# Sketched attention and a mixture of attention experts on one core: sketch matrices decoded ahead of the block transposes, products formed bank by bank, and ten extra matmuls at the start

## The chip, the cores and the metric

One core of one Trainium2 chip runs the kernel. The metric is the time of one execution on the device, in microseconds (us), as the median of several runs. A profile is a trace of one execution. The engines are TensorE (PE; PEld is its weight load), VectorE (DVE), ScalarE (ACT), GpSimd (POOL) and SyncE (SP), which only issues transfers (DMAs); ACT and POOL issue some too. Each engine takes its instructions strictly in the order in which they stand in its own queue.

## The reference

Batch is 4, there are 4 heads, 1088 tokens, head width 32. `S1` and `S2` are two 8 x 32 sketch matrices in double precision; everything else is float32.

```python
def phi(x):                                   # x: one head, S1 and S2 project 32 -> 8
    a = np.einsum('rd,bhsd->bhsr', S1, x)
    b = np.einsum('rd,bhsd->bhsr', S2, x)
    return np.einsum('bhsi,bhsj->bhsij', a, b).reshape(*x.shape[:-1], 64)
q_p, k_p = phi(q), phi(k)
kv = einsum('bhsf,bhsd->bhfd', k_p, v);  z = k_p.sum(axis=2)
x  = (q_p @ kv) / (q_p @ z + 1e-6)            # heads side by side: (B, 1088, 128)
# four experts on x, top 2 of 4 by the logits x @ w_gate, softmax weights w:
for e in range(4):
    a  = softmax(causal(scale * (x @ wq[e]) @ (x @ wk[e]).T))
    out += gate(w, e) * (a @ (x @ wv[e]) @ wo[e])
```

## The kernel before, in words

**Tiling.** A batch is 1088 tokens in NJ = 9 blocks of 128 (the last has 64). Its inputs are `kin`, `qin`, `vin` and `vtl`. VectorE turns `kin` and `qin` in 32 x 32 squares into `kT` and `qT` (L220 to L223: 1024 columns of k, the last 64 columns of k, all of q). `SKW` is the sketch matrix that both are multiplied with: a 128-row block-diagonal matrix, one 32-row block for each head, in two float32 parts (NS = 2), a high and a low one.

**Sketch.** `sketch` (L228) takes four blocks to one PSUM bank, so k and q have three banks each (4, 4 and 1 blocks): matmuls into `kps` or `qps` (L235), a copy by ScalarE of the high part into `kab` or `qab` (L239), and VectorE's addition of the low part (L241). One float32 matmul is two passes in the trace.

**Products.** After all three banks, `products` (L243) forms the 64 features of each token and head: one instruction per head of 128 x 576 elements into `kp` or `qp` (L248). In batch 0 VectorE has three of the four of k and two of q, GpSimd the others; in batches 1 to 3 GpSimd has all.

**Rest of the preparation.** `kvs` (L265) multiplies `kp` with v (copied to `vp` by GpSimd, L217) to `kv`; `turn_features` (L278) transposes `qp` on TensorE into `tq`, evacuated to `qpT`; `numer` (L287) multiplies `qpT` with `kvz` to `num`; VectorE divides (L292 to L294) to `xs`; `turn_x` (L302) transposes to `tx`, evacuated to `xT`. `project` (L312) then makes the experts' `qk` out of `xT`.

**Attention.** For each batch, units of scores, softmax, transposes, values and output follow (`units`). `gates` (L461) has GpSimd make `rb`, which TensorE transposes as `rt` (L468) before values can be scaled. TensorE's order is written out by hand (`manual_schedule`): the pieces of the next batch's preparation are strewn between the units by costs that add up. The other engines' order is set by the tile scheduler, which places each instruction by its own estimate of when it can run. `prepare(0)` runs with nothing to overlap it.

**Start.** The sketch matrices arrive as 64-bit numbers in `S_raw`, 16 rows for each of four heads, in eight small transfers (L116, four from ACT's queue and four from POOL's). VectorE decodes each double into two floats in 19 short integer and float operations (L130 to L151), turns the result to `ST` (L160) and multiplies by a block mask `blk` to `SKW` (L162).

Of the kernel before, what the change touches and what calls it, by code (L numbers as in the profile page):

```python
# [3 lines left out]

# [15 lines left out]
def kernel(  # L20
# [38 lines left out]
    def const(name, shape, dt=F32):  # L59
        return cp.tile(shape, dt, name=name, tag=name)  # L60
# [35 lines left out]


    NS = 1 if S1.dtype == F32 else 2
    S_sum = const("S_sum", [128, NS, 32])
    blk = const("blk", [128, H])  # L100
    nc.gpsimd.memset(blk, 0.0)
    for h in range(H):
        nc.gpsimd.memset(blk[32 * h : 32 * h + 32, h : h + 1], 1.0)
    if NS == 1:
        nc.vector.memset(S_sum, 0.0)
        for x, s in enumerate((S1, S2)):
            for h in range(H):
                nc.scalar.dma_start(out=S_sum[32 * h + R * x : 32 * h + R * x + R, 0, :], in_=s)
        load(0)
    else:  # L110
        raw = const("S_raw", [128, 32, 2], I32)
        nc.vector.memset(raw, 0)
        for x, s in enumerate((S1, S2)):
            for h in range(H):
                eng = (nc.scalar, nc.gpsimd)[h % 2]
                eng.dma_start(out=raw[32 * h + R * x : 32 * h + R * x + R].rearrange("p d w -> p (d w)"),  # L116
                              in_=s.bitcast(I32))
        load(0)

# [38 lines left out]
    ST = const("ST", [128, NS, 32])  # L158
    SKW = const("SKW", [128, NS, 2, H, R])
    nc.vector.transpose(ST.rearrange("p n d -> p (n d)"), S_sum.rearrange("p n d -> p (n d)"))  # L160
    for n in range(NS):
        nc.vector.tensor_tensor(  # L162
            out=SKW[:, n], in0=ST[:, n, 0 : 2 * R].rearrange("p (x r) -> p x r", x=2)[:, :, None, :].to_broadcast([128, 2, H, R]),
            in1=blk[:, None, :, None].to_broadcast([128, 2, H, R]), op=ALU.mult)
    NB = 8 // NS

    nc.gpsimd.memset(kT[:, S:], 0.0)
# [33 lines left out]
    def prepare(b):  # L201
# [14 lines left out]
        def begin():  # L216
            nc.gpsimd.tensor_copy(vp[:, 0:n, :, 0:D].rearrange("p j h d -> p h j d"), vin)  # L217
            nc.gpsimd.tensor_copy(vp[0:64, n, :, 0:D], vtl)

            nc.vector.transpose(kT[:, 0 : 128 * n].rearrange("p (j g t) -> p j g t", j=n, g=4),  # L220
                                kin[:, 0 : 128 * n].rearrange("p (g j d) -> p j g d", g=4, j=n))
            nc.vector.transpose(kT[:, 128 * n : S], kin[:, 128 * n : S])
            nc.vector.transpose(qT[:, 0:S], qin)  # L223
            if b + 1 < B:
                load(b + 1)

        def sketch(nm, xT_, j0):

            if nm not in abS:
                abS[nm] = p2.tile([128, NJ, 64], F32, tag="ab", name=f"{nm}ab{b}")  # L230
            j1 = min(j0 + NB, NJ)
            w = 64 * NS
            t = bank(f"{nm}ps{b}_{j0}")
            for j in range(j0, j1):
                nc.tensor.matmul(t[:, w * (j - j0) : w * (j - j0) + w], xT_[:, 128 * j : 128 * j + 128],  # L235
                                 SKW.rearrange("p s x h r -> p (s x h r)"), start=True, stop=True)
            t = t[:, 0 : w * (j1 - j0)].rearrange("p (j s m) -> p j s m", s=NS, m=64)
            ab = abS[nm][:, j0:j1]
            nc.scalar.copy(ab, t[:, :, 0])  # L239
            if NS == 2:  # L240
                nc.vector.tensor_tensor(out=ab, in0=ab, in1=t[:, :, 1], op=ALU.add)  # L241

        def products(nm, engines):  # L243

            fp = p2.tile([128, NJ, H, R * R], F32, tag="fp", name=f"{nm}p{b}")
            f4 = abS[nm].rearrange("p j (x h r) -> p j x h r", x=2, r=R)
            for h in range(H):
                engines[h].tensor_tensor(  # L248
                    out=fp[:, :, h].rearrange("p j (x y) -> p j x y", y=R),
                    in0=f4[:, :, 1, h, None, :].to_broadcast([128, NJ, R, R]),  # L250
                    in1=f4[:, :, 0, h, :, None].to_broadcast([128, NJ, R, R]),
                    op=ALU.mult)
            fps[nm] = fp
# [30 lines left out]
        def numer(g):  # L284
            num = bank(f"num{b}_{g}")
            for y in range(6):
                nc.tensor.matmul(num[:, 66 * y : 66 * y + 66], qpT[:, 6 * g + y],  # L287
                                 kvz[:, y % 2].rearrange("p h d -> p (h d)"), start=True, stop=True)
            nu = num[:, 0 : 12 * (D + 1)].rearrange("p (m d) -> p m d", d=D + 1)
            den = p2.tile([128, 12], F32, tag="den", name=f"den{b}_{g}")  # L290
            xs = p2.tile([128, 3, 128], F32, tag="xs", name=f"xs{b}_{g}", bufs=3)
            nc.vector.tensor_scalar_add(den, nu[:, :, D], 1e-6)  # L292
            nc.vector.reciprocal(den, den)
            nc.vector.tensor_tensor(  # L294
                out=xs.rearrange("p x (h d) -> p (x h) d", d=D), in0=nu[:, :, 0:D],
                in1=den[:, :, None].to_broadcast([128, 12, D]), op=ALU.mult)
# [55 lines left out]
        V, G = nc.vector, nc.gpsimd  # L352
        kq, qq = ([V, V, V, G], [V, G, V, G]) if first else ([G] * H, [G] * H)
        wait = (0.9, None)
        sk = {nm: [(0.9, lambda j=j, nm=nm, t=t: sketch(nm, t, j)) for j in range(0, NJ, NB)]
              for nm, t in (("k", kT), ("q", qT))}
# [5 lines left out]
        pieces = [(0.0, begin)] + sk["k"] + [(0.0, lambda: products("k", kq))]  # L362
        pieces += sk["q"] + [(0.0, lambda: products("q", qq)), wait, (2.0, lambda: (kvs(0), kvs(1))), wait, wait]
        pieces += tq[0:3] + nu[0:1] + tq[3:4] + nu[1:2] + tq[4:5] + tx[0:1] + nu[2:3] + tx[1:2] + [wait] + tx[2:3]
        rest = pr[1] + [(0.5, project_tails)]
        if first:
# [292 lines left out]
```

## Time and profile before

| what | us |
|---|---|
| median of 3 runs | 433.3 (432.59 to 437.13) |
| the profiled execution, its own time | 433.48 |
| span of that execution, first to last instruction | 430.9 |
| TensorE busy | 394.8 (92% of the span) |
| VectorE, ScalarE, GpSimd busy | 234.2, 225.3, 63.4 |

The time of an execution is the span and 2.6 us around it. The page gives the span in 40 slices; in the first slice TensorE is idle, and its granted clock, `PEclk`, reads below 10 tenths in the third and fourth slice. A row of the chain of waits has a start, a duration and a name: it is followed back from the last instruction, at each step to what released it. A matmul's own duration includes its way through the array; matmuls in a row overlap, so what one costs is the duration of a row divided by its count.

### The profile page before, as it was taken

Reading aid. Unit: us, or ns where it says so; the run is one execution under the profiler, and the core shown is the slowest. Engines: PE = TensorE matmul, PEld = TensorE weight load, DVE = VectorE, ACT = ScalarE, POOL = GpSimd, SP = SyncE. Lnnn points to the kernel's source line nnn. Section 1 sums busy time; section 2 is a strip of 40 time slices with the busy share of each in tenths; the row PEclk is TensorE's granted clock in tenths of the full one; section 3 lists DMA queues with packets and bytes.
Section 4 is the critical chain, followed back from the end, with each engine's and each line's share of the span. In section 5 each row is a group of like instructions: output and inputs, shape, how many; then the busy total and the mean of one; then the engine's idle time right before and its main releaser. Section 6 shows DMA issues by size and latency. Waiting matters only on the chain.

```text
span 430.9 us, 8172 instructions
## 1 busy us (share of the span) xinstructions
PE 394.8 (92%) x3264; PEld 272.0 (63%) x3264; DVE 234.2 (54%) x495; ACT 225.3 (52%) x564; POOL 63.4 (15%) x99
## 2 busy tenths in 40 slices
PE   0678999999999998999999999999999998999995
PEld 0674676775665765686566576777666575666663
DVE  3673665663675454556355545555566355544552
ACT  1122655556655544565564535656664564566662
POOL 4240036000000046000000018000000000000110
PEclk9988999999999999999999999999999999999999
DMA  7532012100000000000000000000000000000000
GB/s 209 152 116 41 2 52 86 33 14 0 2 13 2 14 5 14 0 14 2 1 14 1 9 9 2 14 0 14 0 14 2 0 14 5 0 14 5 2 12 26
DMA packets 11510, 9.98 MB, mean 23 GB/s; under 512 B 3792, under 2 KB 10448, under 8 KB 11472
## 3 DMA queue, kind: packets, MB, share of 16 engines
q1 hardware_dynamic: 9280, 8.92, 7.4%
q10 hardware_dynamic: 2064, 0.53, 0.6%
q8 instruction: 25, 0.41, 0.4%
q14 instruction: 13, 0.11, 0.1%
q0 software_dynamic: 128, 0.01, 0.0%
HBM read 7.23 MB, written 2.23 MB: 22 GB/s over the span
## 4 chain that ended last, share of the span: by engine, by line
PE 74%; ACT 9%; DVE 8%; issue 3%; POOL 3%; DMA 2%; ACTq 0%; POOLq 0%; DVEq 0%
PE sc L390 17%; PE tp L445 14%; PE av L508 13%; PE qk L312 7%; ACT a L376 7%; PE num L287 3%; PE sc L393 3%; PE po L551 3%; PE kps L235 2%; PE vg L324 2%; PE tq L278 2%; PE av L537 2%; PE sc L413 2%; DVE mx L400 2%; PE rt L468 1%
## 5 line engine op out<-in xcount | busy, mean ns | idle before, releaser
L376 ACT ACTIVATE a<-sc,mx 128x1024 f32<-128x1024 f32 (+7 forms) x136 | 103.1, 763 | 87.3 <-DVE mx L400 47.9
L445 PE MATMUL tp<-ident,a 128*128 128x128 f32 (+1 forms) x648 | 95.1, 277 | 6.3 <-ACT a L376 4.8
L400 DVE TENSOR_REDUCE mx<-sc 128x1 f32<-128x640 f32 (+3 forms) x64 | 62.6, 1019 | 49.0 <-PE sc L393 49.0
L72 ACT COPY aT<-tp 128x512 f32<-128x512 f32 (+1 forms) x122 | 63.2, 540 | 45.6 <-PE tp L445 45.2
L445 PEld LDWEIGHTS tp<-ident,a 128*128 128x128 f32 (+1 forms) x648 | 71.4, 141 | 22.2 <-ACT a L376 9.4
L390 PE MATMUL sc<-qkT 64*128 64x512 f32 (+3 forms) x384 | 80.9, 518 | 0.8 <-ACT a L376 0.8
L508 PE MATMUL av<-aT,vt 128*64 128x256 f32 (+1 forms) x640 | 69.2, 363 | 0.0
L461 POOL TENSOR_TENSOR rb<-gw,r 128x256 f32<-128x256 f32 (+1 forms) x36 | 21.2, 590 | 322.4 <-DVE r L458 253.7
L508 PEld LDWEIGHTS av<-aT,vt 128*64 128x64 f32 x640 | 42.9, 137 | 21.7 <-issue 0.2
L390 PEld LDWEIGHTS sc<-qkT 64*128 64x128 f32 x384 | 32.2, 185 | 31.3 <-issue 26.2
L70 DVE COPY aT<-tp 128x512 f32<-128x512 f32 (+2 forms) x58 | 37.8, 652 | 16.5 <-PE tp L445 15.9
L397 DVE TENSOR_REDUCE mx<-sc 128x2 f32<-128x256 f32 (+3 forms) x32 | 26.2, 820 | 21.8 <-PE sc L393 21.8
L312 PE MATMUL qk<-xT,wqk 128*128 128x512 f32 x64 | 33.0, 632 | 0.9 <-ACT xT L72 0.8
L376 ACT ACTIVATION_READ_ACCUMULATOR a<-sc,mx 128x1 f32 x136 | 27.1, 199 | 0.0
L393 PEld LDWEIGHTS <-identb 128*128 128x128 bf16 x128 | 7.3, 97 | 28.1 <-issue 26.2
L235 PE MATMUL kps<-SKW,kT 128*128 128x128 f32 x72 | 11.7, 317 | 14.2 <-DVE SKW L162 14.2
L324 PE MATMUL vg<-wvg,xT 128*128 128x260 f32 (+1 forms) x72 | 21.4, 396 | 1.1 <-DVE vt L70 0.5
L551 PE MATMUL po<-wo,yT 128*128 128x128 f32 (+1 forms) x144 | 20.5, 282 | 1.3 <-ACT aT L72 0.8
L510 DVE TENSOR_TENSOR yT<-av,rs 128x256 f32<-128x256 f32 x32 | 13.5, 422 | 13.5 <-PE av L508 13.4
L235 PEld LDWEIGHTS kps<-SKW,kT 128*128 128x128 f32 x72 | 10.6, 226 | 14.5 <-DVE SKW L162 14.2
L551 PEld LDWEIGHTS po<-wo,yT 128*128 128x128 f32 (+1 forms) x144 | 17.5, 185 | 3.2 <-ACT aT L72 1.1
L248 POOL TENSOR_TENSOR kp<-kab 128x576 f32<-128x576 f32 x13 | 15.5, 1221 | 24.9 <-DVE kab L241 21.6
(117 smaller groups left out, 415.9 us busy)
## 6 DMA issues: line engine op xcount, KB each, us to landing
kin<-in_k_dram SPq DMA_DIRECT2D x4, 544.0 KB, 3.6
qin<-in_q_dram SPq DMA_DIRECT2D x4, 544.0 KB, 6.0
vin<-in_v_dram SPq DMA_DIRECT2D x16, 128.0 KB, 3.1
out_dram<-ob SPq DMA_DIRECT2D x16, 128.0 KB, 1.8
wqk<-in_moe_wq_dram ACTq DMA_DIRECT2D x1, 128.0 KB, 4.9
wqk<-in_moe_wk_dram ACTq DMA_DIRECT2D x1, 128.0 KB, 5.0
wvg<-in_moe_wv_dram ACTq DMA_DIRECT2D x1, 128.0 KB, 3.1
wo<-in_moe_wo_dram ACTq DMA_DIRECT2D x1, 128.0 KB
```

Of the source, the lines that this page charges most:

```text
L70: nc.vector.tensor_copy(out_, in_)
L72: nc.scalar.copy(out_, in_)
L235: nc.tensor.matmul(t[:, w * (j - j0) : w * (j - j0) + w], xT_[:, 128 * j : 128 * j + 128], SKW.rearrange("p s x h r -> p (s x h r)"), star ...
L312: nc.tensor.matmul(t, wt(a), xT[:, 512 * c : 512 * c + 512], start=True, stop=True)
L324: nc.tensor.matmul(t[0:m, 0 : E * HD + E], xT[:, 128 * j : 128 * j + m], wvg, start=True, stop=True)
L376: nc.scalar.activation(out=dst, in_=src, func=ACTF.Exp, bias=mx, accum_out=z)
L390: nc.tensor.matmul(sc[e][:, c0:c1], qk[rows, g, 128 * i : 128 * i + 128], qk[rows, NG + g, c0:c1], start=True, stop=(c1 < n))
L397: nc.vector.tensor_reduce(mx, t[:, :, 0:n], axis=AX.X, op=ALU.max, negate=True)
L400: nc.vector.tensor_reduce(mx[:, e : e + 1], sc[e][:, 0:n], axis=AX.X, op=ALU.max, negate=True)
L445: nc.tensor.transpose(tp[0:nk, k - k0, :], ats[e][:, 128 * j : 128 * j + nk], ident)
L508: nc.tensor.matmul(av[HD * e : HD * e + HD, lo:256], vt[:, j, c : c + HD], aT[:, 2 * j + e, lo:256], start=(j == 0), stop=(j == 2 * p + 1))
L551: nc.tensor.matmul(po[0:nq, DM * x : DM * x + DM], yT[:, g, 128 * x : 128 * x + nq], wo_sb[:, g], start=(g == 0), stop=(g == NG - 1))
```

## The change

The sketch matrices come in two transfers, not eight, one from SP's queue and one from ACT's, into 32 rows, and the decode works on 32 partitions where it worked on 128. `SKW` is set to zero by GpSimd and its four diagonal blocks are copied out of `ST`, two by VectorE and two by GpSimd; `blk` is gone. A scheduling bound, `issue_after(mark[0])`, holds the block transposes of batch 0 behind the turn to `ST`, and those of batch 1 behind the last division `xs` of batch 0. The products are made in `sketch`, at the end of each bank and for all heads at once (128 x 1024 elements for a bank of four blocks, 128 x 256 for the last): by VectorE alone in batch 0, by GpSimd alone after it. `kab` and `qab` have their two halves apart (`[128, 2, NJ, 32]`). Ten matmuls of `ident` with itself, which nothing reads, stand at the head of TensorE's order.

```diff
-    S_sum = const("S_sum", [128, NS, 32])
-    blk = const("blk", [128, H])
-    nc.gpsimd.memset(blk, 0.0)
-    for h in range(H):
-        nc.gpsimd.memset(blk[32 * h : 32 * h + 32, h : h + 1], 1.0)
...
-        raw = const("S_raw", [128, 32, 2], I32)
-        nc.vector.memset(raw, 0)
-        for x, s in enumerate((S1, S2)):
-            for h in range(H):
-                eng = (nc.scalar, nc.gpsimd)[h % 2]
-                eng.dma_start(out=raw[32 * h + R * x : 32 * h + R * x + R].rearrange("p d w -> p (d w)"),
-                              in_=s.bitcast(I32))
-        load(0)
+    S_sum = const("S_sum", [32, NS, 32])
+    raw = S_sum.rearrange("p n d -> p (n d)") if NS == 1 else const("S_raw", [32, 32, 2], I32)
+    nc.vector.memset(raw, 0.0 if NS == 1 else 0)
+    for x, s in enumerate((S1, S2)):
+        eng = (nc.sync, nc.scalar)[x]
...
+            eng.dma_start(out=raw[R * x : R * x + R].rearrange("p d w -> p (d w)"), in_=s.bitcast(I32))
+    load(0)
...
-    nc.vector.transpose(ST.rearrange("p n d -> p (n d)"), S_sum.rearrange("p n d -> p (n d)"))
-    for n in range(NS):
-        nc.vector.tensor_tensor(
-            out=SKW[:, n], in0=ST[:, n, 0 : 2 * R].rearrange("p (x r) -> p x r", x=2)[:, :, None, :].to_broadcast([128, 2, H, R]),
-            in1=blk[:, None, :, None].to_broadcast([128, 2, H, R]), op=ALU.mult)
+    nc.gpsimd.memset(SKW, 0.0)
+
+    mark = [nc.vector.transpose(ST.rearrange("p n d -> p (n d)"), S_sum.rearrange("p n d -> p (n d)")).ins]
+    for h in range(H):
+        (nc.vector, nc.gpsimd)[h % 2].tensor_copy(
+            SKW[32 * h : 32 * h + 32, :, :, h, :], ST[:, :, 0 : 2 * R].rearrange("d n (x r) -> d n x r", x=2))
...
-            nc.vector.transpose(kT[:, 0 : 128 * n].rearrange("p (j g t) -> p j g t", j=n, g=4),
+            with tc.issue_after(mark[0]) if b < 2 else nullcontext():
+                nc.vector.transpose(kT[:, 0 : 128 * n].rearrange("p (j g t) -> p j g t", j=n, g=4),
...
-                abS[nm] = p2.tile([128, NJ, 64], F32, tag="ab", name=f"{nm}ab{b}")
+                abS[nm] = p2.tile([128, 2, NJ, H * R], F32, tag="ab", name=f"{nm}ab{b}")
+                fps[nm] = p2.tile([128, NJ, H, R * R], F32, tag="fp", name=f"{nm}p{b}")
...
-        def products(nm, engines):
...
-            for h in range(H):
-                engines[h].tensor_tensor(
-                    out=fp[:, :, h].rearrange("p j (x y) -> p j x y", y=R),
...
+            ab = ab.rearrange("p x j (h r) -> p x (j h) r", r=R)
+            n = H * (j1 - j0)
+            (nc.vector if first else nc.gpsimd).tensor_tensor(
+                out=fps[nm][:, j0:j1].rearrange("p j h (x y) -> p (j h) x y", y=R),
+                in0=ab[:, 1, :, None, :].to_broadcast([128, n, R, R]),
+                in1=ab[:, 0, :, :, None].to_broadcast([128, n, R, R]),
+                op=ALU.mult)
...
-            nc.vector.tensor_tensor(
+            last = nc.vector.tensor_tensor(
                 out=xs.rearrange("p x (h d) -> p (x h) d", d=D), in0=nu[:, :, 0:D],
                 in1=den[:, :, None].to_broadcast([128, 12, D]), op=ALU.mult)
+            if first:
+                mark[:] = [last.ins]
...
-        kq, qq = ([V, V, V, G], [V, G, V, G]) if first else ([G] * H, [G] * H)
...
     with tc.manual_schedule(engines={mybir.EngineType.PE}):
+
+        warm = ps_tp.tile([128, 512], F32, tag="tp", name="warm")
+        for _ in range(10):
+            nc.tensor.matmul(warm[:, 0:128], ident, ident, start=True, stop=True)
```

VectorE's queue at the start, before: the decode (`S_` names) stands between the transposes of k and q (five of its 19 operations are shown).

```order
L198 TENSOR_SCALAR wqk<-wqk 128x256
L220 STREAM_TRANSPOSE kT<-kin 128x1024
L132 TENSOR_SCALAR S_ex<-S_raw 128x32
...
L222 STREAM_TRANSPOSE kT<-kin 128x64
L132 TENSOR_SCALAR S_ex<-S_ex 128x32
L135 TENSOR_TENSOR S_ma<-S_ma,S_lw 128x32
L223 STREAM_TRANSPOSE qT<-qin 128x1088
L130 TENSOR_SCALAR S_ex<-S_ex 128x32
...
L135 TENSOR_TENSOR S_sum<-S_lead,S_last 128x32
L160 STREAM_TRANSPOSE ST<-S_sum 128x64
L162 TENSOR_TENSOR SKW<-ST,blk 128x64 x2
```

The same place now, where the whole decode and `ST` come first:

```order
L190 TENSOR_SCALAR wqk<-wqk 128x256
L123 TENSOR_SCALAR S_ex<-S_raw 32x32
...
L126 TENSOR_TENSOR S_sum<-S_lead,S_last 32x32
L153 STREAM_TRANSPOSE ST<-S_sum 32x64
L213 STREAM_TRANSPOSE kT<-kin 128x1024
L155 COPY SKW<-ST 32x4x8 x2
L215 STREAM_TRANSPOSE kT<-kin 128x64
L216 STREAM_TRANSPOSE qT<-qin 128x1088
```

The long transpose of k moved behind the decode, ahead of the two copies into `SKW`; the transpose of q moved behind everything that the first sketch matmul needs.

VectorE's queue at batch 0's products, before; the transposes in it belong to batch 1.

```order
L241 TENSOR_TENSOR kab_189<-kab_189,kps_8_204 128x64
L248 TENSOR_TENSOR kp_208<-kab_189 128x9x64 x3
L241 TENSOR_TENSOR qab_213<-qab_213,qps_0_214 128x256
L241 TENSOR_TENSOR qab_213<-qab_213,qps_4_221 128x256
L241 TENSOR_TENSOR qab_213<-qab_213,qps_8_228 128x64
L220 STREAM_TRANSPOSE kT<-kin 128x1024
L248 TENSOR_TENSOR qp_232<-qab_213 128x9x64 x2
L222 STREAM_TRANSPOSE kT<-kin 128x64
L223 STREAM_TRANSPOSE qT<-qin 128x1088
L70 COPY qpT_175<-tq_8_288 128x512
```

The same place now:

```order
L235 TENSOR_TENSOR kab_191<-kab_191,kps_0_193 128x2x128
L235 TENSOR_TENSOR kab_191<-kab_191,kps_4_201 128x2x128
L239 TENSOR_TENSOR kp_192<-kab_191 128x1024 x2
L235 TENSOR_TENSOR kab_191<-kab_191,kps_8_209 128x2x32
L235 TENSOR_TENSOR qab_214<-qab_214,qps_0_216 128x2x128
L239 TENSOR_TENSOR kp_192<-kab_191 128x256
L239 TENSOR_TENSOR qp_215<-qab_214 128x1024
L235 TENSOR_TENSOR qab_214<-qab_214,qps_4_224 128x2x128
L235 TENSOR_TENSOR qab_214<-qab_214,qps_8_232 128x2x32
L239 TENSOR_TENSOR qp_215<-qab_214 128x1024
L239 TENSOR_TENSOR qp_215<-qab_214 128x256
L70 COPY qpT_177<-tq_8_288 128x512
```

Batch 1's transposes left this place for one behind the last `xs` of batch 0, just ahead of the copy of the first `qk` bank. The first product of k stands behind the sums of two banks, not of one.

GpSimd's queue in batch 1, before:

```order
L461 TENSOR_TENSOR rb_0_1_546<-gw_173,r_0_1_543 128x256
L248 TENSOR_TENSOR kp_577<-kab_528 128x9x64 x4
L248 TENSOR_TENSOR qp_652<-qab_582 128x9x64 x3
L461 TENSOR_TENSOR rb_1_0_631<-gw_173,r_1_0_628 128x256
L248 TENSOR_TENSOR qp_652<-qab_582 128x9x64
```

and now:

```order
L450 TENSOR_TENSOR rb_0_1_549<-gw_175,r_0_1_546 128x256
L239 TENSOR_TENSOR kp_529<-kab_528 128x1024 x2
L239 TENSOR_TENSOR kp_529<-kab_528 128x256
L239 TENSOR_TENSOR qp_582<-qab_581 128x1024 x2
L239 TENSOR_TENSOR qp_582<-qab_581 128x256
L450 TENSOR_TENSOR rb_1_0_634<-gw_175,r_1_0_631 128x256
```

The gate's `rb` still stands behind products of q, but each product now needs only its own bank's sum, not all three. In batch 0 GpSimd has no products any more. TensorE's order is the same, row for row, but for the ten matmuls at its head.

## Rows read from the trace of the kernel before

**Rows 1.** Stretches: start:end, length, busy of PE, PEld, DVE, ACT, POOL, granted clock, DMA share.

```profile
14.20:19.20 5.00, 5.00 (x23) 5.00 (x24) 1.25 (x5) 0.96 (x3) 0.16 (x1) 1.00 0.71 141
26.50:31.00 4.50, 4.49 (x26) 4.50 (x27) 2.02 (x4) 1.17 (x2) 1.01 (x2) 0.62 0.65 193
37.00:41.00 4.00, 4.00 (x6) 1.70 (x7) 0.69 (x1) 0.36 (x1) 0.00 (x0) 0.57 0.00 0
100.00:200.00 100.00, 95.81 (x808) 65.55 (x806) 54.46 (x115) 54.84 (x139) 15.65 (x19) 1.00 0.02 7
...
23.70:26.50 2.80, 0.34 (x2) 0.16 (x2) 2.80 (x5) 0.42 (x2) 2.80 (x3) 1.00 0.03 9
```

**Rows 2.** Chain of waits, first 50 us: start, duration, what.

```profile
1.91 4.65 DMA S_raw<-in_S_dram
...
8.67 0.18 DVE S_ex L132
...
9.50 1.22 DVE qT L223
...
11.26 0.99 DVE S_ma L135
...
13.77 0.37 DVE SKW L162 x2
...
14.18 3.79 PE kps L235 x16
...
18.40 0.56 DVE kab L241 x2
...
18.99 3.07 DVE kp L248 x3
22.06 0.79 DVE qab L241 x3
22.85 1.16 DVE kT L220
...
28.86 1.98 PE num L287 x12
...
31.29 1.29 PE num L287 x12
...
36.92 5.40 PE qk L312 x8
```

**Rows 3.** Single instructions of POOL and DVE in time: start, duration, what, idle before.

```profile
1.94 2.24 POOL L116 DMA_DIRECT2D S_raw<-in_S_dram  x4
4.75 0.29 POOL masks.py:199 TENSOR_SCALAR_AFFINE_SELECT ident<-ident 128x128 f32<-128x128 f32 x1
11.16 1.05 POOL L217 COPY vp<-vin 128x1024 f32<-128x1024 f32 x1 [5.38 <-DMA vtl<-in_v_dram]
...
5.71 0.29 DVE L198 TENSOR_SCALAR wqk<-wqk 128x256 f32<-128x256 f32 x1 [4.77 <-DMA wqk<-in_moe_wq_dram]
38.98 0.69 DVE L70 COPY qkT<-qk 128x512 f32<-128x512 f32 x1 [3.51 <-PE qk L312]
```

**Rows 4.** One matmul pass or product: count, min/median/max ns, first and last start.

```profile
L235 PE MATMUL kps<-SKW,kT x18: 421/421/581, 14.2 to 18.0; 128*128 128x128 f32 x18
...
L235 PE MATMUL qps<-SKW,qT x7: 275/275/275, 20.3 to 20.9; 128*128 128x128 f32 x7
...
L278 PE MATMUL tq<-ident,qp x9: 397/421/421, 26.8 to 28.4; 128*128 128x128 f32 x9
...
L248 POOL TENSOR_TENSOR kp<-kab x13: 1177/1177/1738, 19.0 to 260.8; 128x576 f32<-128x576 f32 x13
L248 DVE TENSOR_TENSOR kp<-kab x3: 745/758/1729, 19.0 to 21.3; 128x576 f32<-128x576 f32 x3
```

**Rows 5.** TensorE in time, the product of k with v in batch 0.

```profile
21.13 2.60 PE L265 MATMUL kv<-vp,kp 128*64 128x33 f32 x72
```

**Rows 6.** Who TensorE waited for, 60 to 300 us: total, times, longest.

```profile
PE rt L468 <- POOL rb L461: 3.1, 4, 1.3
```

More of the change, by code (lines that the diff above doesn't have):

```diff
@@ L2 @@
 import math
-from contextlib import ExitStack
+from contextlib import ExitStack, nullcontext
 import concourse.bass as bass
@@ L98 @@
     NS = 1 if S1.dtype == F32 else 2
-    S_sum = const("S_sum", [128, NS, 32])
-    blk = const("blk", [128, H])
-    nc.gpsimd.memset(blk, 0.0)
-    for h in range(H):
-        nc.gpsimd.memset(blk[32 * h : 32 * h + 32, h : h + 1], 1.0)
-    if NS == 1:
-        nc.vector.memset(S_sum, 0.0)
-        for x, s in enumerate((S1, S2)):
-            for h in range(H):
-                nc.scalar.dma_start(out=S_sum[32 * h + R * x : 32 * h + R * x + R, 0, :], in_=s)
-        load(0)
-    else:
-        raw = const("S_raw", [128, 32, 2], I32)
-        nc.vector.memset(raw, 0)
-        for x, s in enumerate((S1, S2)):
-            for h in range(H):
-                eng = (nc.scalar, nc.gpsimd)[h % 2]
-                eng.dma_start(out=raw[32 * h + R * x : 32 * h + R * x + R].rearrange("p d w -> p (d w)"),
-                              in_=s.bitcast(I32))
-        load(0)
+    S_sum = const("S_sum", [32, NS, 32])
[3 more added lines that the diff above has]
+        eng = (nc.sync, nc.scalar)[x]
+        if NS == 1:
+            eng.dma_start(out=raw[R * x : R * x + R], in_=s)
+        else:
+            eng.dma_start(out=raw[R * x : R * x + R].rearrange("p d w -> p (d w)"), in_=s.bitcast(I32))
+    load(0)
+    if NS == 2:
         S_hi, S_lo = S_sum[:, 0], S_sum[:, 1]
         lo, hi = raw[:, :, 0], raw[:, :, 1]
-        ex, sg, ma, lw = (const(f"S_{n}", [128, 32], I32) for n in ("ex", "sg", "ma", "lw"))
-        lead, last, ok = (const(f"S_{n}", [128, 32]) for n in ("lead", "last", "ok"))
+        ex, sg, ma, lw = (const(f"S_{n}", [32, 32], I32) for n in ("ex", "sg", "ma", "lw"))
+        lead, last, ok = (const(f"S_{n}", [32, 32]) for n in ("lead", "last", "ok"))
         SHR, SHL, AND, OR = (
@@ L156 @@
         both(S_lo, lead, last, ALU.add)
-    ST = const("ST", [128, NS, 32])
+    ST = const("ST", [32, NS, 32])
     SKW = const("SKW", [128, NS, 2, H, R])
-    nc.vector.transpose(ST.rearrange("p n d -> p (n d)"), S_sum.rearrange("p n d -> p (n d)"))
-    for n in range(NS):
-        nc.vector.tensor_tensor(
-            out=SKW[:, n], in0=ST[:, n, 0 : 2 * R].rearrange("p (x r) -> p x r", x=2)[:, :, None, :].to_broadcast([128, 2, H, R]),
-            in1=blk[:, None, :, None].to_broadcast([128, 2, H, R]), op=ALU.mult)
+    nc.gpsimd.memset(SKW, 0.0)
[3 more added lines that the diff above has]
+            SKW[32 * h : 32 * h + 32, :, :, h, :], ST[:, :, 0 : 2 * R].rearrange("d n (x r) -> d n x r", x=2))
     NB = 8 // NS
@@ L218, in begin @@
             nc.gpsimd.tensor_copy(vp[0:64, n, :, 0:D], vtl)
-            nc.vector.transpose(kT[:, 0 : 128 * n].rearrange("p (j g t) -> p j g t", j=n, g=4),
-                                kin[:, 0 : 128 * n].rearrange("p (g j d) -> p j g d", g=4, j=n))
-            nc.vector.transpose(kT[:, 128 * n : S], kin[:, 128 * n : S])
-            nc.vector.transpose(qT[:, 0:S], qin)
+            with tc.issue_after(mark[0]) if b < 2 else nullcontext():
+                nc.vector.transpose(kT[:, 0 : 128 * n].rearrange("p (j g t) -> p j g t", j=n, g=4),
+                                    kin[:, 0 : 128 * n].rearrange("p (g j d) -> p j g d", g=4, j=n))
+                nc.vector.transpose(kT[:, 128 * n : S], kin[:, 128 * n : S])
+                nc.vector.transpose(qT[:, 0:S], qin)
             if b + 1 < B:
@@ L236, in sketch @@
                                  SKW.rearrange("p s x h r -> p (s x h r)"), start=True, stop=True)
-            t = t[:, 0 : w * (j1 - j0)].rearrange("p (j s m) -> p j s m", s=NS, m=64)
-            ab = abS[nm][:, j0:j1]
-            nc.scalar.copy(ab, t[:, :, 0])
+            t = t[:, 0 : w * (j1 - j0)].rearrange("p (j s x m) -> p s x j m", s=NS, x=2, m=H * R)
+            ab = abS[nm][:, :, j0:j1]
+            nc.scalar.copy(ab, t[:, 0])
             if NS == 2:
-                nc.vector.tensor_tensor(out=ab, in0=ab, in1=t[:, :, 1], op=ALU.add)
-        def products(nm, engines):
-            fp = p2.tile([128, NJ, H, R * R], F32, tag="fp", name=f"{nm}p{b}")
-            f4 = abS[nm].rearrange("p j (x h r) -> p j x h r", x=2, r=R)
-            for h in range(H):
-                engines[h].tensor_tensor(
-                    out=fp[:, :, h].rearrange("p j (x y) -> p j x y", y=R),
[L250 to L253, printed above, removed]
+                nc.vector.tensor_tensor(out=ab, in0=ab, in1=t[:, 1], op=ALU.add)
+            ab = ab.rearrange("p x j (h r) -> p x (j h) r", r=R)
[5 more added lines that the diff above has]
+                op=ALU.mult)
         kvt = []
@@ L350, in gate @@
                 nc.vector.tensor_copy(gw8[64 * g : 64 * g + 64], gw[0:64, NJ - 1, 2 * g : 2 * g + 2])
-        V, G = nc.vector, nc.gpsimd
-        kq, qq = ([V, V, V, G], [V, G, V, G]) if first else ([G] * H, [G] * H)
         wait = (0.9, None)
@@ L361, in prepare @@
         pr = [[(0.9, lambda a=a, c=c: project(a, c)) for a in (0, 2, 1, 3)] for c in range(2)]
-        pieces = [(0.0, begin)] + sk["k"] + [(0.0, lambda: products("k", kq))]
-        pieces += sk["q"] + [(0.0, lambda: products("q", qq)), wait, (2.0, lambda: (kvs(0), kvs(1))), wait, wait]
+        pieces = [(0.0, begin)] + sk["k"] + sk["q"] + [wait, (2.0, lambda: (kvs(0), kvs(1))), wait, wait]
         pieces += tq[0:3] + nu[0:1] + tq[3:4] + nu[1:2] + tq[4:5] + tx[0:1] + nu[2:3] + tx[1:2] + [wait] + tx[2:3]
```

## The prediction

> **What bounds the kernel now.** I read the stretches first. From 100 to 200 us TensorE is busy 95.8 of 100 us at full granted clock [rows 1]; its order is unchanged but for ten matmuls, so there only its few waits can shrink, and whatever ends the preparation of batch 0 sooner moves the whole rest forward. So the change is worth what it does before batch 0's projections start at 36.92, and the chain of waits [rows 2] is the view for that: the sketch matrices' transfer, the decode from 8.67, `SKW`, the sketch matmuls from 14.18, VectorE's sums and products to 26.4 (with a transpose of batch 1 in the middle), `num` from 28.86, `qk` from 36.92. TensorE starts nothing before 14.18.
>
> The clock is read third. [...] Ahead of the first fall TensorE had worked 0.34 of 2.80 us [rows 1]. In 14.2 to 19.2 the column reads 1.00, but the passes tell otherwise: 421 ns each, as in the stretch known to be low, and 275 from 20.3 on [rows 4]. The sketch starts at the low level too; the column shows no change before its first record.
>
> **The change part by part. A, the start of the sketch.** Before, ACT's transfers waited on landed by 6.56, POOL's later, and the decode began at 8.67 [rows 2]. Two transfers are left, each second in its queue, behind `kin` and the first half of `wqk`. Issued no later than 1.91 and with the row's 4.65 us [rows 2], they land by 6.6; VectorE is busy with `wqk` until 6.0 [rows 3]. I take 6.3, ends 6.0 and 7.0 (the latter if 544 KB of `kin` in front cost SP's one half a microsecond more). The decode to the start of `SKW` took 5.1 us, with the transpose of q (1.22) inside and one operation that took 0.99 where its like takes 0.18 [rows 2], while GpSimd copied `vp` [rows 3]: 5.1 - 1.22 - 0.81 = 3.1 without both. The 32 partitions save nothing I can see, since the free size is the same. So `ST` is there at 9.4, the transpose of k behind it takes 1.16, `SKW`'s two copies 0.37 as its two products did [rows 2]: first matmul at 10.9 instead of 14.18, **-3.3 us** (ends -3.6 and -2.6). GpSimd's two copies of `SKW` run beside k's transpose. What is late next is that transpose.
>
> **The ten matmuls.** GpSimd made `ident` by 5.04, with 2.24 us of transfer issues ahead of it that go [rows 3]; so about 2.6 now (estimate). Twenty passes at 3.79/18 = 0.21 us each [rows 2, 4] end at 6.8, and then TensorE has nothing until 10.9: 4.1 us of idling, longer than the 2.8 us after which the trace shows the low level [rows 1]. I price them at nothing: they run while TensorE would wait anyway, and the sketch starts at the low level as before.
>
> **B, from the first sketch matmul to `num`.** Before: 28.86 - 14.18 = 14.7 us. Now VectorE's queue sets it. Counting from the first matmul, the sums of two banks of k are done at 4.6 (the first two of three; 18.40 and the row's count [rows 2]). A product of 576 elements takes 0.745 alone [rows 4], so 1024 in proportion 1.32 and 256 0.33. Two products of k: 7.2. The sum of k's last bank and of q's first (0.6 of the 0.79 that three took [rows 2]): 7.8. Products 0.33 and 1.32: 9.4. Two sums: 10.0. Products 1.32 and 0.33: 11.7. TensorE starts `kv` at 7.2, takes 2.60 [rows 5], is done at 9.8, transposes the eight pieces for which q's first product is there (0.11 us each, as 1.29/12 in `num` at the high level [rows 2]: 10.7), waits for q's second product at 11.3, transposes four more and starts `num` at 11.8. Batch 1's transposes, 1.16 of them on this chain [rows 2], have gone from it. In front of them now is VectorE's idle time before the first `qk` copy, 3.51 us [rows 3], and three transposes of together some 2.6 us (1.16 and 1.22 are the two long ones) fit; without that cover they would delay one copy by what is over, and `project` has three more banks to go on with. One collision is new: GpSimd copies batch 1's `vp` (1.05 us [rows 3]) when `kv` ends, at 9.8, just when VectorE begins q's second product. The nearest row is the 0.99 instead of 0.18: up to 0.8 to 1.0 us. I take 12.0 (11.8 and a fifth of that), ends 11.5 (a product of 1024 at its 1.1 us, if 0.2 of the 0.745 is fixed) and 12.8: **-2.7 us** (-3.2 and -1.9).
>
> [...]
>
> **C and D, the clock.** With the gap before the transposes gone, or down to about a microsecond, the fall at 26.5 should go: `num`'s first twelve passes took 1.98 instead of 1.29 [rows 2], **-0.7 us** (at least 0). The fall at 37 follows the pauses between the last `num` and `qk`, which the change leaves; I leave it: 0. If it went, 4.0 x (1 - 0.57) = 1.7 us [rows 1].
>
> **E, batches 1 to 3.** TensorE waits for `rb` 3.1 us in four waits [rows 6], since `rb` stands in GpSimd's queue behind products that all wait for the last bank. Per element the products cost the same, 1.18 us for 576 [rows 4], but two thirds of them can now start one or two banks sooner, and a matrix takes 4.7 us in all: more than the longest wait of 1.3. I take **-2.0 us**, ends 0 and -2.7.
>
> The smaller transfer count, `blk`'s loss and the sets of `SKW` cost nothing: GpSimd has nothing due until the copy at 11.16 [rows 3]. The copies and sums into the split `kab` have the same count of elements.
>
> Sum: 3.3 + 2.7 + 0.7 + 2.0 = 8.7. Span 430.9 - 8.7 = 422.2, with the 2.6 us around it **424.8**. All good ends, the 1.7 of D among them: 11.9, 421.6; all bad ends: 4.5, 429.0. The profiled execution (433.48) stands 0.2 above the median of the three runs, so nothing is corrected for.
>
> **The rivals.** *The clock is better than I think* (27 in 100). Either the ten matmuls do hold the level to the sketch: then 16 passes before the second bank's sum go at about half of 0.21, 1.6 us, 423.2; against it speaks the 4.1 us gap. Or the fall before `qk` does not come: 1.7 us, 423.1; for it speaks that the pauses there now fall at other times. Both: 421.5.
>
> *The gains are eaten at their edges* (10): the transfer behind `kin` lands late, the `vp` copy costs all its time, and the waits for `rb` stay because other waits follow at once: 2.6 + 1.9 + 0.7 = 5.2, 428.3.
>
> *No difference* (6): the bad ends, and the level falls once more in the shorter, no denser preparation, 1.7 us: 430.7. This includes that the change does not do what it says: `kin` and `wqk` still precede the sketch matrices, and if these land with `qin`, decode and sketch stay where they were.
>
> *Slower* (3): GpSimd's new products. In batches 1 to 3 each `rb` stands behind all three products of q. If a 1024-element product over (block, head) pairs cost twice the 2.04 ns per element of now [rows 4], the 4608 elements of a batch would take 9.4 us more, `rb` would be some 7 us late, three times: 424.8 + 2.0 + 21 = 448. It decides from about 3.4 ns per element on, where the lost 13 us exceed the gain by the 1% below. Against it: the new view has fewer strides than the old, and the output is dense.
>
> **The numbers.** My forecast gets 54 in 100. The range reaches from half a microsecond below the case in which both clock rivals hold to the bad ends: 421.0 to 429.0. A measurement of this kernel tells about 1% (4.3 us) from no change; a gain over that is in my case and the first two rivals: 91. Within: 6. Slower: 3.
>
> **What would show it.** First sketch matmul near 10.9, decode starting near 6.3 and no operation of it near 1 us. Sketch passes at 421 ns after a pause of some 4 us behind the ten matmuls (275 would prove me wrong there). `num` starting near 22.9 and its first twelve passes in 1.3 us; `qk` near 30.2 (36.92 less A to C), its first passes at granted 0.50. Waits for `rb` of well under 3.1 us. I am wrong if `qk` starts after 32, if the products on GpSimd take over 2.5 us for 1024 elements, or if TensorE after 60 us waits for something new.

## The result and the profile after

The changed kernel takes **419.46 us** in the median of four runs (417.13 to 420.57), the kernel before 435.22 in its own four; the ratio is 0.963 (95% interval 0.954 to 0.972). In a second series, further below, it is 0.961 (0.958 to 0.965). The profiled execution of the change took 420.57 us with a span of 418.7. It is faster, as forecast, but by more than the range allowed (421.0 to 429.0).

Three things make up the difference. Against the *profiled* execution of the kernel before (span 430.9) the change saves 12.2 us where 8.7 were forecast. The time around the span is 1.9 us in this execution and 1.7 to 1.9 in most others of either kernel; the 2.6 that I had read from one execution is an exception. And the profiled execution of the change is the longest of its four; the median is 1.1 below it.

The execution of the kernel before that I started from was not a typical one either: of the 27 runs of the kernel before beside the experiments, 6 took 432.3 to 433.0 us at a mean granted clock of 0.99, like the profiled one, and 21 took 436.5 to 438.6 at 0.975 to 0.979.

The chain of waits of the changed kernel (start, duration, what), which answers to [rows 2]:

```profile
5.31 0.16 DVE S_ex L123
...
7.76 0.24 DVE ST L153
...
9.52 3.77 PE kps L229 x16
...
14.14 2.27 DVE kp L239 x2
...
16.68 2.29 PE kv L255 x72
18.98 1.67 PE tq L268 x12
20.65 1.29 PE num L277 x12
...
28.03 5.40 PE qk L304 x8
```

The decode starts at 5.31 in place of 8.67 and its last result is turned at 7.76 in place of 13.41; the sketch starts at 9.52 in place of 14.18. In the chain before, the turn to `ST` is

```profile
13.41 0.26 DVE ST L160
```

After the products of k the chain stays on TensorE to `num`: `kv`, the transposes and `num` follow each other without a gap. `qk` starts at 28.03, 8.9 us sooner, and takes the same 5.40.

Its stretches (start:end, length, busy of PE, PEld, DVE, ACT, POOL, granted clock, DMA share), which answer to [rows 1]:

```profile
9.50:13.00 3.50, 3.48 (x16) 3.50 (x17) 1.87 (x4) 0.37 (x1) 0.71 (x1) 1.00 0.85 238
28.50:31.80 3.30, 3.30 (x5) 1.35 (x4) 1.23 (x2) 0.32 (x1) 0.00 (x0) 0.50 0.79 237
```

The first fall, at 26.5 before, is gone (the granted clock reads 1.00 from 14 to 26 us); the one ahead of `qk` is still there (0.50 from 28.5 to 31.8). The passes of k's sketch, and its ten matmuls at the start (line 552), still tell the low level where the column reads 1.00: 421 ns, as the transposes `tq` of the kernel before from 26.8 on [rows 4], where its granted clock reads 0.50 (27 to 30 us):

```profile
L229 PE MATMUL kps<-SKW,kT x18: 421/421/553, 9.5 to 13.3; 128*128 128x128 f32 x18
L552 PE MATMUL warm<-ident x20: 421/421/582, 2.4 to 6.6; 128*128 128x128 f32 x20
```

After 45 us TensorE waits for `rb` once:

```profile
PE rt L457 <- POOL rb L450: 0.7, 1, 0.7
```

Over the same part of the kernel before, the four waits of [rows 6] and one behind them:

```profile
PE rt L468 <- POOL rb L461: 3.8, 5, 1.3
```

The ledger from the two chains, span against span:

| part | before | after | saved | forecast |
|---|---|---|---|---|
| A: start to first sketch matmul | 14.18 | 9.52 | 4.7 | 3.3 |
| B: from there to `num` | 14.68 | 11.13 | 3.5 | 2.7 |
| C: `num` to `qk` | 8.06 | 7.38 | 0.7 | 0.7 |
| D: first eight `qk` passes | 5.40 | 5.40 | 0 | 0 |
| E: the rest | 388.6 | 385.3 | 3.3 | 2.0 |

### The profile page after: what moved, and what is told of

Its sections match the earlier page's. It is cut to its first block, busy times and chain, and to the rows that moved or that the text cites. A ratio compares the mean times of both kernels' runs of the same rounds, so it can differ in the third digit from the quotient of the medians.

```text
span 418.7 us, 8188 instructions
## 1 busy us (share of the span) xinstructions
PE 396.7 (95%) x3284; PEld 274.1 (65%) x3284; DVE 232.1 (55%) x496; ACT 224.9 (54%) x564; POOL 55.9 (13%) x84
## 4 chain that ended last, share of the span: by engine, by line
PE 80%; ACT 9%; DVE 6%; issue 3%; DMA 1%; POOL 0%; POOLq 0%; ACTq 0%; DVEq 0%
PE sc L379 18%; PE tp L434 15%; PE av L497 14%; PE qk L304 7%; ACT a L365 6%; PE sc L382 3%; PE po L540 3%; PE num L277 3%; PE kps L229 2%; PE vg L316 2%; PE kv L255 2%; PE av L526 2%; PE tq L268 2%; PE sc L402 2%; DVE mx L389 2%
## 5 line engine op out<-in xcount | busy, mean ns | idle before, releaser
L70 DVE COPY aT<-tp 128x512 f32<-128x512 f32 (+2 forms) x58 | 37.7, 652 | 16.2 <-PE tp L434 15.7
L382 PE MATMUL sc<-cmask,identb 128*128 128x128 bf16 x128 | 18.3, 224 | 0.0
L304 PEld LDWEIGHTS qk<-xT,wqk 128*128 128x128 f32 x64 | 11.1, 199 | 10.2 <-issue 5.9
L277 PE MATMUL num<-kvz,qpT 128*128 128x66 f32 x144 | 17.4, 271 | 0.0
```

The costliest lines, as they stand in the source:

```text
L70: nc.vector.tensor_copy(out_, in_)
L304: nc.tensor.matmul(t, wt(a), xT[:, 512 * c : 512 * c + 512], start=True, stop=True)
L382: nc.tensor.matmul(sc[e][:, 128 * i : n], identb, cmask, start=False, stop=True)
```

## The experiments

Each kernel was profiled once and timed beside the kernel before; the change and the kernel before were profiled once more at the end. Spans are compared with those of the changed kernel: 415.3 to 418.7 in its first four runs, 417.1 to 419.9 in six more.

**Half of A: the queue.** `y1_pool_queue` differs from the change in one line:

```diff
-        eng = (nc.sync, nc.scalar)[x]
+        eng = (nc.gpsimd, nc.gpsimd)[x]
```

> The changed kernel with its two sketch transfers issued from GpSimd's queue, where half of the eight were before. My theory: each issue takes GpSimd 0.5 us and lands some 5 us later, the decode starts at 7 to 7.6 in place of 5.31, the sketch 1.7 to 2.3 us later, span near 420.7. Rival: the decode waits for wqk anyway, which lands at 5.1, and nothing moves.

Median 423.85 us; the profiled span is 421.1. GpSimd's two issues, then VectorE's first decode operation with the idle time before it, then the sketch on TensorE:

```profile
1.37 1.22 POOL L107 DMA_DIRECT2D S_raw<-in_S_dram  x2 [0.17 <-issue]
...
8.53 0.17 DVE L123 TENSOR_SCALAR S_ex<-S_raw 32x32 int32<-32x32 int32 x1 [2.82 <-DMA S_raw<-in_S_dram]
...
12.75 3.62 PE L229 MATMUL kps<-SKW,kT 128*128 128x128 f32 x18 [4.35 <-POOL lower L175]
```

The decode starts 3.2 us later than in the change, and the sketch by as much. That is nearly the whole 3.36 us by which the change had brought the decode forward. The direction was mine, the size not: the issues are over at 2.6, so it is not late issues that make 8.53. The transfer itself lands 5.9 us after them, where the one from ACT's queue, issued at 1.24, had landed by 5.3. So two transfers in place of eight do not help by themselves; leaving GpSimd's queue does. Eight transfers from the other two queues were not run.

**The other half of A: the bound.** `x5_batch0_free` lets batch 0's transposes stand where the scheduler wants them:

```diff
-            with tc.issue_after(mark[0]) if b < 2 else nullcontext():
+            with tc.issue_after(mark[0]) if b == 1 else nullcontext():
```

> The changed kernel without the bound that holds batch 0's transposes behind the decode; the scheduler then puts the long transpose of k ahead of the decode and that of q inside it. My theory: decode ends 2.8 to 3 us later (1.1 + 0.2 + 1.2 and the wait for k), k's transpose no longer follows it (1.1 back): the sketch starts near 11.3 in place of 9.5, span near 420.5. Rival: the two transfers alone made the start earlier, and the sketch starts within 0.5 us of 9.5.

Median 421.94 us, profiled span 419.3. Its chain of waits:

```profile
1.59 7.32 DMA qin<-in_q_dram
...
8.94 1.31 DVE qT L216
10.25 0.06 DVE S_ma L126
...
12.20 1.86 PE kps L229 x7
```

The sketch starts at 12.20, 2.7 us later than in the change, so the transfers alone do not make the start. The loss is larger than expected, since q's transpose, put into the middle of the decode, waits for `qin` until 8.9 with seven decode operations and the turn to `ST` behind it. The span loses less (its granted clock reads 1.00 from 28 to 34 us: it did not fall ahead of `qk`, whose eight passes took 3.70).

**B and E from the change's side.** `x3_products_at_end` has the old products in the new kernel:

```diff
-            (nc.vector if first else nc.gpsimd).tensor_tensor(
-                out=fps[nm][:, j0:j1].rearrange("p j h (x y) -> p (j h) x y", y=R),
...
+            for h in range(H):
...
+                engines[h].tensor_tensor(
+                    out=fps[nm][:, :, h].rearrange("p j (x y) -> p j x y", y=R),
```

> The changed kernel with the products made as before the change: after all three banks, one instruction per head, VectorE and GpSimd sharing batch 0, GpSimd alone later. My theory: batch 0 loses about 1.2 us at num (products cannot start before the third bank), and TensorE's waits for rb come back in batches 1 to 3 from 0.7 to about 3 us: together 3.6, span near 422.3. Rival: the rb waits went because of the new start, not because of the products; then only 1.2, span near 420.

Median 428.01 us, profiled span 426.6: 7.9 worse than the change, not 3.6. TensorE in batch 0:

```profile
20.68 0.33 PE L270 MATMUL tq<-ident,qp 128*128 128x128 f32 x1 [0.67 <-POOL qp L241]
22.32 2.61 PE L270 MATMUL tq<-ident,qp 128*128 128x128 f32 x11 [1.32 <-POOL qp L241]
24.72 1.82 PE L279 MATMUL num<-kvz,qpT 128*128 128x66 f32 x12
```

It waits twice for GpSimd's two products of q, and behind these pauses its clock is low again (granted 0.52 from 22 to 24 us and 0.63 from 24 to 26; eleven transposes in 2.61 us, where the change has twelve in 1.74). `num` starts 15.0 us after the sketch, not 11. The waits for `rb` total 3.8 us again, and from `qk` on it takes 394.0 us where the change takes 390.7. Both gains belong to the products; the rival, that the `rb` waits went with the new start, falls. I had left out GpSimd's part as the slow one, and the low clock behind its pauses.

Why GpSimd is slow here stands in the durations of q's products:

```profile
L241 DVE TENSOR_TENSOR qp<-qab x2: 757/1244/1730, 18.8 to 19.5; 128x576 f32<-128x576 f32 x2
L241 POOL TENSOR_TENSOR qp<-qab x2: 1685/1716/1746, 18.9 to 20.6; 128x576 f32<-128x576 f32 x2
```

Alone, such a product takes 0.75 us on VectorE and 1.18 on GpSimd [rows 4]. Side by side only VectorE's first one keeps its time; the others take 1.7. In the products of k, which do not overlap in this kernel, both keep their time (0.75 and 1.18); in the kernel before these overlap too (0.76, 1.73 and 0.75 on VectorE, 1.74 on GpSimd). So the change gains in batch 0 by two things at once: products start by banks, and VectorE makes them alone. `x3_products_at_end` takes both back, and no run here separates them.

**E alone.** `y2_products_at_end_1to3` keeps batch 0 bank by bank and returns batches 1 to 3 to one instruction per head:

```diff
+            if not first:
+                return
...
+        ends = [[] if first else [(0.0, lambda nm=nm: products(nm, [G] * H))] for nm in "kq"]
```

> The changed kernel with the products of batches 1 to 3 made per head after all banks on GpSimd, as before the change; batch 0 stays bank by bank. My theory: batch 0 is as in the changed kernel (qk at 28.0), and from there to the end 2.4 to 3.1 us come back with the waits for rb. Rival: the stretch after qk stays within 0.5 us of 390.7.

Median 424.38 us, profiled span 422.6, and its waits:

```profile
PE rt L470 <- POOL rb L463: 3.8, 5, 1.3
```

`qk` starts at 28.32 and from there it is 394.3 us, 3.6 more than the change. That is all the waits of batches 1 to 3 (3.1) and half a microsecond, above the 2.4 to 3.1 that I expected; E's good end (2.7) was too small.

**The products without the new start.** `z2_products_only` is the kernel before with the new `sketch`:

```diff
-        def products(nm, engines):
...
+            (nc.vector if first else nc.gpsimd).tensor_tensor(
```

> The kernel before with the new products alone: bank by bank, VectorE in batch 0 and GpSimd later; transfers, decode, bounds and start as before. My theory: the sketch starts at 14.2 as before, num follows it after some 11 us in place of 14.7, the waits for rb fall from 3.8 to 0.7, and the span is near 424 (430.9 less 3.6 and 3.3). Rival: without the new start GpSimd and VectorE get in each other's way as before, and less than 4 us are gained.

Median 429.36 us (spans 426.0 to 427.9, the profiled one 427.7). TensorE in batch 0, then its wait for `rb`, then two late stretches (columns as in [rows 1]):

```profile
14.43 3.81 PE L236 MATMUL kps<-SKW,kT 128*128 128x128 f32 x18 [14.43 <-DVE SKW L162]
...
25.23 1.45 PE L284 MATMUL num<-kvz,qpT 128*128 128x66 f32 x12
...
34.02 5.40 PE L309 MATMUL qk<-xT,wqk 128*128 128x512 f32 x8 [0.85 <-ACT xT L72]
```

```profile
PE rt L462 <- POOL rb L455: 0.9, 1, 0.9
```

```profile
355.60:359.00 3.40, 3.40 (x13) 2.04 (x13) 0.69 (x1) 0.59 (x1) 0.00 (x0) 0.50 0.04 11
420.50:423.90 3.40, 3.40 (x16) 2.21 (x16) 0.42 (x1) 0.37 (x1) 0.00 (x0) 0.50 0.00 0
```

`num` starts 10.8 us after the sketch, and the waits for `rb` fall to 0.9: both need no new start. Still the span is 3.7 us over what I expected, and only 3.2 under the profile of the kernel before; the rival's number came, though not for its reason. Some 0.7 us of this come ahead of `qk`: without the bound, batch 1's transposes stand among the divisions, and from `num` to `qk` it takes 8.8 us where the change takes 7.55 by the same rows. The other 3.0 are lost behind `qk`, where it takes 393.7 us, no better than the 394.0 before. This is the clock: up to the transposes `tp` at 354.25, which the change begins at 347.99, this kernel falls only 0.3 us further behind the change than it was at `qk`; over the two falls above, the distance grows from 6.3 to 9.0. So E's gain is there until 354 us and then lost again. Why the level falls there I have no experiment on.

**Batch 1's transposes.** `x4_batch1_free` removes only that bound:

```diff
-            with tc.issue_after(mark[0]) if b < 2 else nullcontext():
+            with tc.issue_after(mark[0]) if b < 1 else nullcontext():
```

> The changed kernel without the bound that holds batch 1's transposes behind the last division of batch 0. The scheduler then puts k's long transpose before the copy of qpT and q's ahead of the first xs. My theory: xs of the first group is late by about 2.6 us less the slack of 0.7 that it has, and qk starts 1 to 2 us later than at 28.03. Rival: other work hides it and qk starts within 0.3 us of 28.03.

Median 421.18 us, profiled span 418.8. `qk` starts at 28.09, `num` at 20.08: 8.0 us between them against 7.55 in the change, by the same rows. The cost is half a microsecond, less than I said and more than nothing; here it hid behind a higher clock at the start of the sketch (18 passes of k in 2.97 us, see the ten matmuls).

**The ten matmuls.** `x1_no_warm` has none:

```diff
-        warm = ps_tp.tile([128, 512], F32, tag="tp", name="warm")
-        for _ in range(10):
-            nc.tensor.matmul(warm[:, 0:128], ident, ident, start=True, stop=True)
```

> The changed kernel without its ten matmuls at the start. My theory: they bought nothing, because TensorE idles 2.5 us between them and the sketch. The sketch starts near 9.5 us with passes of 421 ns as in the changed kernel, and the span stays within 1 us of its 418.7. Rival: they bring the rise of the clock forward. Then without them more passes run at 421 ns and num starts 1 to 1.6 us later, span near 420.

Median 420.3 us, spans 417.3 to 419.0, and its passes:

```profile
L229 PE MATMUL kps<-SKW,kT x18: 421/421/553, 9.8 to 13.6; 128*128 128x128 f32 x18
L229 PE MATMUL qps<-SKW,qT x18: 274/275/422, 13.8 to 15.8; 128*128 128x128 f32 x18
```

The passes of k are those of the change's first profile (421/421/553), and the spans lie inside its own: a gain in time is not shown. But the ten matmuls are not without effect in every execution. `x4_batch1_free` starts like the change, with the same ten, ended 2.8 us before the sketch, and has

```profile
L229 PE MATMUL kps<-SKW,kT x18: 275/276/422, 9.9 to 12.4; 128*128 128x128 f32 x18
```

Its k passes are at the high level, its q passes then partly at the low one (2.97 and 3.12 us for 18, in the change 4.18 and 2.79), and `num` follows the sketch after 10.2 us in place of 11.0. One execution of a kernel does not tell what ten matmuls do.

`x2_warm20` and `y3_warm20_fill` have twenty, the second also three and four more in TensorE's pauses ahead of `qk`:

```diff
-        for _ in range(10):
+        for _ in range(20):
...
-            pieces, rest = pieces + pr[0], vg + rest
+            pieces.insert(len(pieces) - 1, (0.0, lambda: idle(13)))
+            pieces, rest = pieces + [(0.0, lambda: idle(24))] + pr[0], vg + rest
```

> The changed kernel with twenty matmuls at the start in place of ten, so that TensorE works until the sketch matrices are ready. My theory: the clock rises in the meantime and holds, the sketch passes take 275 ns from the first one, and num starts some 1.6 us sooner; qk still begins at the low level. Span near 417. Rival: the extra matmuls run at the low level past 9.5 us, delay the sketch by about 1.3 us, and nothing or less than nothing is gained.

> Twenty matmuls at the start, and three more ahead of batch 0's last transposes of x and four ahead of qk, into scratch memory, where TensorE waits anyway. My theory: the clock stays at its high level from the sketch on, the first eight qk passes take 3.4 to 3.5 us in place of 5.4, and with the earlier sketch the span is near 415. Rival: the level falls before qk all the same, or the fillers delay the transposes by what they take (0.7 us), and nothing is gained over twenty matmuls alone.

The profiled execution of `x2_warm20` took 637 us at a mean granted clock of 0.56 and says nothing on this; the other three took 418.85 to 420.64 (spans 417.1 to 418.9), which is inside the change's own. `y3_warm20_fill`: median 418.11 us, profiled span 416.6. `z3_best` adds a bound to it that holds each bank's product in batch 0 ahead of the next bank's sum:

```diff
-            if NS == 2:
+            with tc.issue_after(held[-1]) if first and held else nullcontext():
                 nc.vector.tensor_tensor(out=ab, in0=ab, in1=t[:, 1], op=ALU.add)
...
+            held.append(made.ins)
```

> Twenty matmuls at the start and the seven fillers, and in batch 0 each bank's product held ahead of the next bank's sum in VectorE's queue. My theory: the first product starts near 11.4 in place of 12.4 (with the sketch at the high level), num about 1 us sooner than the 19.3 of the version without this bound, span near 415. Rival: the sums of q wait behind the products and TensorE's banks fill up; nothing is gained.

> The changed kernel, unchanged, beside the version with fillers and bounds. My theory: spans between 415.3 and 418.7 as before, by whether the clock falls ahead of qk; the other version is 2 to 3 us faster in the median. Rival: the two agree within 1 us.

TensorE in `z3_best`, and below it three stretches of it (columns as above):

```profile
2.40 6.33 PE L560 MATMUL warm<-ident 128*128 128x128 f32 x40 [2.40 <-POOL ident masks.py:199]
9.61 2.25 PE L230 MATMUL kps<-SKW,kT 128*128 128x128 f32 x18 [0.87 <-POOL lower L175]
...
15.13 2.29 PE L257 MATMUL kv<-vp,kp 128*64 128x33 f32 x72 [1.26 <-POOL vp L211]
...
19.17 1.45 PE L279 MATMUL num<-kvz,qpT 128*128 128x66 f32 x12
...
26.71 3.70 PE L311 MATMUL qk<-xT,wqk 128*128 128x512 f32 x8
```

```profile
9.60:13.80 4.20, 4.19 (x36) 4.07 (x36) 3.99 (x7) 1.36 (x5) 1.42 (x2) 1.00 0.63 162
26.70:30.40 3.70, 3.70 (x11) 1.50 (x10) 1.71 (x2) 1.17 (x2) 0.00 (x0) 1.00 0.67 205
360.00:380.00 20.00, 18.68 (x175) 13.70 (x171) 8.77 (x20) 12.81 (x32) 1.01 (x2) 0.91 0.03 7
```

With twenty matmuls and a pause of 0.87 us instead of 2.5 the high level does reach the sketch: all 36 passes are over in 4.2 us, and `qk` takes 3.70. So the preparation can be kept at the high level from the sketch on. What it buys is small. `num` comes only 1.3 us sooner than in the change's profile, since now `kv` waits for GpSimd's copy of `vp`, and the bound of `z3_best` gains 0.1 over `y3_warm20_fill` (19.26). With the 1.7 us at `qk` the lead is 3.0 us there, and 2.2 at the end: in this execution the level falls between 360 and 380, which takes 0.8 back. Timed together, `z3_best` has 418.46 us (ratio 0.959, 0.956 to 0.963) and the change 419.44 (0.961, 0.958 to 0.965): the intervals overlap, and a gain of a microsecond is not shown, let alone the 2 to 3 that I expected.

**The kernel before, once more.**

> The kernel before, unchanged, profiled once more: its runs beside the others fall at 432.4 us with a mean granted clock of 0.99 or at 437.5 with 0.975. My theory: in the longer runs the fall of the clock in the preparation of batch 0 lasts longer or comes once more, and qk starts later than 36.92 by most of the 5 us. Rival: the difference lies after 60 us, or in the transfers at the start.

It took 436.47 us, span 434.7, one of the longer executions. Its stretch after the first matmuls of the preparation, and `qk`:

```profile
27.20:44.20 17.00, 15.68 (x63) 12.81 (x62) 5.63 (x13) 3.62 (x6) 0.31 (x2) 0.50 0.36 98
```

```profile
40.60 5.50 PE L312 MATMUL qk<-xT,wqk 128*128 128x512 f32 x8 [0.84 <-ACT xT L72]
```

The sketch starts at 14.16 as in the first profile. But once the clock has fallen behind TensorE's pause of 23.7 to 26.5, it stays at the low level for 17.0 us, not 3.4 (the mean of 0.62 over 4.5 us in [rows 1] is 3.4 us at 0.50), through `num` and the transposes to `qk`, which starts at 40.60, not 36.92: 3.7 of the 3.8 us between the two spans. The change takes that pause away, and none of its two profiles has this stretch. So against the commoner executions of the kernel before the change is worth about 4 to 5 us more than against the one that I had; most of them have a granted clock of 0.975, and of these none was profiled.

## Why the prediction was wrong

- **What bounds the kernel** held: all of A to C arrived at `qk` and, with E, at the end; TensorE's order after it shows no new wait.
- **A was mis-sized: -3.3 forecast, -4.7 measured**, beyond its good end of 3.6. I let the decode begin at 6.3, between the landing of `S_raw` (6.6) and the end of `wqk` (6.0). Both came sooner: `S_raw` had landed by 5.31, and the decode began there, as soon as `wqk` (5.10) let VectorE go. I had priced the two transfers by the 4.65 us of one that ACT issued among eight, and had no reason for the late 8.67 but that POOL's landed "later"; `y1_pool_queue` shows that GpSimd's queue is the slow one (decode at 8.53 in place of 5.31). And the decode took 2.7 to the end of `ST`, not 3.1, though a decode operation on 32 partitions took about what one on 128 had (medians 0.17 and 0.18 us).
- **B was mis-sized: -2.7, measured -3.5**, beyond its good end of 3.2. The step that failed is that TensorE would wait for q's second product until 11.3. A product of 1024 elements takes 1.13 us, not 1.32 in proportion (my lower guess of 1.1 was right), so this one was there at 10.35, and TensorE ran from `kv` to `num` without a wait: 0.3 us. `kv` began at 7.16 as forecast (7.2) and took 2.29, not 2.60: another 0.3. The last 0.2 is the collision with `vp`. It came, but on an instruction that delays nothing:

```profile
18.72 2.41 DVE L239 TENSOR_TENSOR qp<-qab 128x1024 f32<-128x1024 f32 x2
...
19.67 1.18 POOL L209 COPY vp<-vin 128x1024 f32<-128x1024 f32 x1 [6.11 <-PE tq L268]
```

These are VectorE's last two products, and GpSimd's copy inside them. The first product had begun 0.95 us before the copy and took its 1.22; the small one behind it took 1.27 where its like takes 0.42, and the copy 1.18 for 1.05. I had the order wrong: I let the copy start ahead of q's second product. The 0.8 us for that order is an estimate of mine, from the operation of [rows 2] that began 0.10 us into the copy of [rows 3] (0.99 where its like takes 0.18).
- **The ten matmuls at nothing**: no gain in time is shown by `x1_no_warm`. The reason that I gave did not come true as it stood: the pause behind them was 2.5 us, not 4.1, and so not longer than the 2.8 that I compared it with. The rival that the level holds to the sketch did not come in the change's profile, came for the passes of k in `x4_batch1_free`, and comes with twenty.
- **C** was right (0.7). **D** was right for the profile (5.40); in the second profile of the change the level does not fall there, and `qk` takes 3.70, as it does in `x1_no_warm`, `x5_batch0_free` and `y1_pool_queue` behind the same pause of some 0.85 us. So it is not decided by the kernel alone. This half of the rival *the clock is better than I think* holds in some executions; that D came out at 0 in the first profile is in part luck.
- **E was mis-sized: -2.0, measured -3.3**, `y2_products_at_end_1to3` alone 3.6. I took 2.0 of the 3.1 us of [rows 6], a discount for which I had no row; but all four waits were queueing behind products, and all four went.
- **The time around the span was mis-sized: 2.6 forecast, 1.9 measured.** It was read from one execution; 1.7 to 1.9 is usual.
- **The base** was one of two lengths of the kernel before. I set the profiled execution 0.2 us above a median of three runs and corrected nothing, though one of the three was 437.13 and most runs lie there. This does not move the forecast time, which starts from the profiled execution; it makes the measured ratio (0.963) better than 419.46 against 433.3 (0.968). Most of the spread of those three runs was a second length of the same stretch, as far as one profile of it shows.
- Each single step went the forecast way, and A, B and E each came out past its good end; that is why the sum left the range. Of the rivals, *eaten at their edges*, *no difference* and *slower* did not come; a product of 1024 elements takes GpSimd 1.95 us, which per element is no more than before (1.90 ns against 2.04).

## What to carry to other kernels

A chain that ends in a short table (here a decode of 32 rows) should not stand behind long work in the same in-order queue, nor wait for a transfer issued through the slowest queue: both halves were needed, and either alone gave back some 3 us of 4.7. Split work that others queue behind by the piece that feeds it, as the products by bank: the 3.3 us in batches 1 to 3 came from starting sooner, on the same engine and with the same count of elements. In batch 0 (3.5 us) the same split came together with leaving GpSimd out, whose products and VectorE's had stretched each other. And where the few runs of a kernel spread by 1%, profile it twice before costing a change against one trace.

## What the runs showed of the hardware

- A 2 KB transfer issued from GpSimd's queue at 1.4 to 2.6 us landed at 8.5; one issued from ScalarE's at 1.24 had landed by 5.3.
- The level of TensorE's clock after a pause is not fixed by the program: after the same pause of 23.7 to 26.5 us it stayed at 0.50 for 3.4 us in one execution and for 17.0 in another, and TensorE was busy 15.7 of these 17.0. Why it did not rise there stays open.
- Falls come and go between executions. Ahead of `qk`, behind the same pause of some 0.85 us, the level falls in the change's first profile and not in its second. A late fall, between 355 and 380 us, shows in `x1_no_warm` and `y3_warm20_fill` (granted clock 0.83 from 360 to 370) and `z3_best` (0.91 from 360 to 380), which have none ahead of `qk`, and in `z2_products_only` (0.50 from 355.6 to 359), which has one; `z4_change_again` and `x5_batch0_free` have neither (1.00 from 28 to 400). In `z3_best` it cost 0.8 us. What decides is open.
- A product of 576 elements takes VectorE 0.75 us and GpSimd 1.18. Side by side, in the kernel before, VectorE's first one, which began 0.05 us ahead of GpSimd's, took 0.76, GpSimd's 1.74 and VectorE's second 1.73.
